# Retention and two feed-forward layers on one core: each layer's first step by eight block products, and second-stage blocks fetched four steps ahead

## The chip, the cores and the metric
The kernel runs on one core of a Trainium2 chip. The metric is the device time of the whole program in microseconds (us), median of several runs. TensorE (PE) multiplies into PSUM, VectorE (DVE), ScalarE (ACT) and GpSimd (POOL) work on SBUF, and SyncE (SP) issues nearly all DMAs, in the order in which the program names them.

## The reference
`x` is the output of a retention layer (2 batches, 8 heads, 768 positions, head size 64), laid out as 1536 tokens by 512 features. Two feed-forward layers follow, with 2048 inner features:

```
state = gamma * state + k_t (outer) v_t ;  y_t = scale * q_t . state
x  = silu(x @ w_in1) @ w_out1             # 512 -> 2048 -> 512
out = leaky_relu_0.01(x @ w_in2) @ w_out2
```
All in fp32; the weights reach the kernel as 64-bit words.

## The kernel before, in words
**Retention** runs as 12 chunks of 128 positions (`j`): `queries` and `keys` scale on POOL, `scores` and `values` multiply on PE, `masked` masks on DVE, `store_x` writes the chunk into `x`. `load_att` fetches four chunks ahead.

**Numbers.** A matrix product is made of three products of high and low parts (`TERMS`): `halves(h, l, s)` makes the high part on ACT and the low part on DVE. A weight block is **converted** from its words in pieces: `words` (ACT, two instructions), `clamp` (DVE, two), `signed` (DVE, which also calls for the next load), `low` (DVE). It then lies in one of three tiles `r` (the list `rt`), and is written to a scratch in DRAM (`keep_w`, read back by `fetch_w`) or split at once. `sums` makes four sums of a block on POOL into the tile `sf`; `split_a` and `split_s` split the block and its sums.

**First stage of a layer** (x times w_in, 8 steps, `Step`): the 1536 tokens lie in four sets of 384. Set 0 and set 2 (`xa[0]`, `xa[1]`) are the upper, set 1 and set 3 (`xb[0]`, `xb[1]`) the lower halves of two pairs; index `p` (a lane) is the pair. A step does a two by two block product by seven block products instead of eight (Winograd's scheme), six matmuls of 128x384 for each product and lane. Four of the seven need the transformed inputs `T4` (`tt`), which `rest_t` (POOL) and `split_t` (ACT, DVE) make, two need the split sums. Each product adds to another in PSUM, so copies (`copy`, ACT) and adds (`add`, DVE) stand between them. `begin` runs step 0 product by product and lane by lane, and the first product of step 1 inside it; `rest` runs the steps after it, in which the next step's first product stands ahead. `up_tasks` puts conversions and splits between the products. `keep` writes a step's results (1.5 MB) to DRAM.

**Second stage** (times w_out): three groups of 512 tokens by 8 blocks of results, 24 steps `n`, each of 24 matmuls of 128x512 (`down`). `fetch_g` brings a block back into one of the three tiles `ct`, `split_g` splits it two steps ahead of its use. `todo` spreads the conversions of later weights over these steps. `finish_x` (layer 0) turns a group's PSUM into the next layer's x, `finish_out` (layer 1) stores it.

Order on each engine is that of the program text; engines wait for each other by semaphores alone. Every DMA named above but the first constants is on SP's queue.

Of the kernel before, what the change touches and what calls it, by code (L numbers as in the profile page):

```python
# [28 lines left out]
N = 384  # L29
# [12 lines left out]
def retention_moe_kernel(ctx: ExitStack, tc: tile.TileContext, att, w1, w2, cst, out):  # L42
# [28 lines left out]
    rt = [sb.tile([128, 2, 512], I32, name=f"r{i}") for i in range(3)]  # L71
    u = sb.tile([128, 2, 512], I32, name="u")
    sf = sb.tile([128, 4, 256], F32, name="sf")
# [212 lines left out]


# [52 lines left out]
    A22, A11, A12 = range(3)  # L340
# [24 lines left out]
    class Step:  # L365
# [46 lines left out]
        def done(self):  # L412
            free.extend(W.pop(self.w))
# [5 lines left out]
    def fetch_g(layer, s, i):  # L419
        n = len(fetched)  # L420
        fetched.append(n)
        t = sf.rearrange("p (a b) n -> p a (b n)", a=2) if n % (SETS * Q) == 0 else ct[(n % (SETS * Q) - 1) % 3]
# [34 lines left out]
    with tc.manual_schedule():  # L457
        nc.scalar.dma_start(out=cs, in_=cst[:, 0:ncs])
        g2 = rt[2][0:1].bitcast(F32)
# [50 lines left out]
        def pieces(w, end=keep_w):  # L510
# [6 lines left out]
            8: lambda: (low(wa), sums(wa, (0,)), split_t(0, 0)), 9: lambda: (sums(wa, (1,)), split_a(wa)),  # L517
            10: lambda: (sums(wa, (2, 3)), rest_t(0), words(wb)), 11: lambda: (split_s(wa), rest_t(1)),
        }
        for j in range(NJ):  # L520
# [25 lines left out]
        def up_tasks(layer, k):  # L546
            t = [[] for _ in range(8)]
            at = lambda n, *f: t[n].extend(f)
            if layer == 0 and k < 2:
                wd = first_w[3]  # L550
                if k == 0:
                    at(0, lambda: split_t(1, 0))
                    at(1, lambda: split_t(0, 1))
                    at(2, lambda: clamp(wb))
                    at(3, lambda: signed(wb), lambda: split_t(1, 1))
                    at(4, lambda: (low(wb), sums(wb)))
                    at(5, lambda: split_a(wb), lambda: words(wc))
                    at(6, lambda: clamp(wc))
                    at(7, lambda: split_s(wb))
                else:  # L560
                    at(0, lambda: signed(wc))
                    at(1, lambda: (low(wc), sums(wc)), lambda: words(wd))
                    at(2, lambda: split_a(wc))
                    at(3, lambda: split_s(wc), lambda: clamp(wd))
                    at(5, lambda: signed(wd))
                    at(6, lambda: (low(wd), sums(wd)))
# [24 lines left out]
            if k == 0:  # L591
                at(0, lambda: split_t(1, 0))
# [199 lines left out]
```

## Time and profile before

| | us |
|---|---|
| median of 3 runs (628.49 to 631.32) | 629.25 |
| the profiled execution | 629.81 |
| its span, first to last instruction | 628.0 |
| PE busy / mean granted clock | 572.3 / 0.959 |
| DVE busy, ACT busy, POOL busy | 341.3, 286.0, 107.6 |

The profiled execution lies 0.56 us above the median, and its span is 1.81 us shorter than its time. Busy time of PE counts pipelined matmuls and can hide slow ones; the stages have to be read one by one.

### The profile page before, as it was taken

Reading aid. Unit: us, or ns where it says so; the run is one execution under the profiler, and the core shown is the slowest. Engines: PE = TensorE matmul, PEld = TensorE weight load, DVE = VectorE, ACT = ScalarE, POOL = GpSimd, SP = SyncE. Lnnn points to the kernel's source line nnn. Section 1 sums busy time; section 2 is a strip of 40 time slices with the busy share of each in tenths; the row PEclk is TensorE's granted clock in tenths of the full one; section 3 lists DMA queues with packets and bytes.
Section 4 is the critical chain, followed back from the end, with each engine's and each line's share of the span. In section 5 each row is a group of like instructions: output and inputs, shape, how many; then the busy total and the mean of one; then the engine's idle time right before and its main releaser. Section 6 shows DMA issues by size and latency. Waiting matters only on the chain.

```text
span 628.0 us, 7949 instructions
## 1 busy us (share of the span) xinstructions
PE 572.3 (91%) x3222; PEld 503.5 (80%) x3222; DVE 341.3 (54%) x359; ACT 286.0 (46%) x337; POOL 107.6 (17%) x102
## 2 busy tenths in 40 slices
PE   9968699999998699899989788999999699999996
PEld 7757589998997487687767688999998488888884
DVE  4974846887864375545755756556655361320400
ACT  2222447777763544424634365665565341422301
POOL 2746314333300000000204522212200000000000
PEclk9997879999999799899999798999999899999999
DMA  8980106787757755676557206677735770631501
GB/s 328 380 303 3 67 3 232 255 280 264 273 194 255 256 168 176 225 223 211 170 188 240 109 0 238 238 253 251 254 139 201 280 262 26 235 100 48 187 1 67
DMA packets 35129, 119.09 MB, mean 190 GB/s; under 512 B 3218, under 2 KB 3346, under 8 KB 33044
## 3 DMA queue, kind: packets, MB, share of 16 engines
q1 hardware_dynamic: 34800, 118.24, 54.3%
q8 instruction: 25, 0.41, 0.2%
q10 hardware_dynamic: 292, 0.34, 0.2%
q14 instruction: 12, 0.10, 0.1%
HBM read 80.82 MB, written 37.75 MB: 189 GB/s over the span
## 4 chain that ended last, share of the span: by engine, by line
PE 52%; DMA 16%; DVE 14%; ACT 8%; issue 6%; POOL 3%; SPq 1%; ACTq 0%; DVEq 0%; POOLq 0%
PE p L436 25%; PE p L359 23%; DMA c<-g 9%; DMA scr<-r 3%; ACT w L172 3%; DVE w L173 2%; DVE r L142 2%; DVE r L149 2%; DVE big L392 2%; POOL sf L169 1%; DMA att_b<-att_dram 1%; DVE r L131 1%; DMA sf<-g 1%; DVE tt L173 1%; ACT u L127 1%
## 5 line engine op out<-in xcount | busy, mean ns | idle before, releaser
L359 PE MATMUL p<-tt,w 128*128 128x384 f32 x768 | 149.9, 346 | 13.4 <-ACT c L388 8.3
L359 PEld LDWEIGHTS p<-tt,w 128*128 128x128 f32 x768 | 139.3, 194 | 17.5 <-ACT c L388 11.2
L173 DVE TENSOR_TENSOR w<-c,w 128x1024 fp32r<-128x1024 f32 x46 | 56.8, 1236 | 137.0 <-ACT w L172 136.9
L436 PE MATMUL p<-w,wt 128*128 128x512 f32 x432 | 105.7, 404 | 10.8 <-ACT wt L172 5.0
L436 PEld LDWEIGHTS p<-w,wt 128*128 128x128 f32 x432 | 83.2, 194 | 33.2 <-DVE w L173 5.8
L436 PE MATMUL p<-wt,w 128*128 128x512 f32 x432 | 101.8, 397 | 7.6 <-ACT wt L172 6.0
L436 PEld LDWEIGHTS p<-wt,w 128*128 128x128 f32 x432 | 82.4, 191 | 26.6 <-ACT wt L172 6.4
L172 ACT ACTIVATE w<-c 128x1024 fp32r<-128x1024 f32 x46 | 48.7, 1061 | 107.4 <-DMA c<-g 70.0
L359 PE MATMUL p<-xa,w 128*128 128x384 f32 x384 | 74.4, 342 | 5.7 <-ACT c L388 5.3
L359 PEld LDWEIGHTS p<-xa,w 128*128 128x128 f32 x384 | 68.7, 192 | 6.9 <-ACT c L388 5.9
L436 PE MATMUL p<-w,w 128*128 128x512 f32 x288 | 69.2, 398 | 3.4 <-ACT w L172 1.8
L388 ACT ACTIVATE c<-p 128x768 f32<-128x768 f32 (+1 forms) x54 | 39.8, 741 | 65.8 <-PE p L359 63.2
L436 PEld LDWEIGHTS p<-w,w 128*128 128x128 f32 x288 | 54.9, 192 | 16.7 <-DVE w L173 2.8
L392 DVE TENSOR_TENSOR big<-p,c 128x768 f32<-128x768 f32 (+1 forms) x54 | 46.7, 864 | 39.4 <-PE p L359 23.3
L169 POOL TENSOR_TENSOR sf<-r 128x256 f32<-128x256 f32 x32 | 36.6, 1164 | 172.9 <-DVE r L149 64.9
L127 ACT ACTIVATE u<-ws 128x1024 int32<-128x1024 uint32 x32 | 36.5, 1140 | 16.2 <-DVE r L149 16.2
L149 DVE CUSTOM_DVE_ANT_0 r<-r,u 128x2048 uint16<-128x2048 uint16 x32 | 41.2, 1287 | 1.1
L125 ACT ACTIVATE r<-ws 128x1024 f32<-128x1024 f32 x32 | 36.5, 1139 | 9.3 <-DMA scr<-r 9.2
L142 DVE SCALAR_TENSOR_TENSOR r<-ws,r 128x1024 int32<-128x1024 int32 x32 | 39.6, 1237 | 0.4
L173 DVE TENSOR_TENSOR w<-sf,w 128x1024 fp32r<-128x1024 f32 x18 | 22.4, 1246 | 29.4 <-ACT w L172 29.4
L359 PE MATMUL p<-xb,w 128*128 128x384 f32 x192 | 37.3, 342 | 0.0
L359 PEld LDWEIGHTS p<-xb,w 128*128 128x128 f32 x192 | 34.6, 192 | 0.0
(74 smaller groups left out, 457.1 us busy)
## 6 DMA issues: line engine op xcount, KB each, us to landing
ws<-w_dram SPq DMA_DIRECT2D x64, 512.0 KB, 5.4
g<-big SPq DMA_DIRECT2D x16, 1536.0 KB, 5.8
c<-g SPq DMA_DIRECT2D x46, 512.0 KB, 6.8
att_a<-att_dram SPq DMA_DIRECT2D x18, 512.0 KB, 7.0
scr<-r SPq DMA_DIRECT2D x18, 512.0 KB, 6.4
r<-scr SPq DMA_DIRECT2D x18, 512.0 KB, 7.3
att_b<-att_dram SPq DMA_DIRECT2D x6, 512.0 KB, 8.4
out_dram<-big SPq DMA_DIRECT2D x11, 256.0 KB, 2.1
```

Of the source, the lines that this page charges most:

```text
L125: nc.scalar.activation(out=r.bitcast(F32), in_=t[:, :, :, 1].bitcast(F32), func=AF.Abs)
L127: nc.scalar.activation(out=u, in_=t[:, :, :, 0].bitcast(U32), func=AF.Copy, scale=2.0 ** -29)
L131: nc.vector.tensor_scalar(out=r.bitcast(F32), in0=r.bitcast(F32), scalar1=MIN_NORMAL, scalar2=MAX_NORMAL, op0=ALU.max, op1=ALU.min,)
L142: nc.vector.scalar_tensor_tensor(out=r, in0=t[:, :, :, 1], scalar=-0x40000000, in1=r, op0=ALU.bitwise_and, op1=ALU.bitwise_or)
L149: nc.vector.tensor_tensor(out=r, in0=r, in1=u, op=ALU.add)
L169: nc.gpsimd.tensor_tensor(out=o, in0=a, in1=b, op=op)
L172: nc.scalar.activation(out=h, in_=s, func=AF.Copy)
L173: nc.vector.tensor_tensor(out=l, in0=s, in1=h.bitcast(F32), op=ALU.subtract)
L359: nc.tensor.matmul(out=o, lhsT=a[:, ta, k * 128:k * 128 + 128], rhs=rhs(p, tb, k), start=(begin and m == 0), stop=(end and m == 5), skip_g ...
L388: nc.scalar.activation(out=ct[n][:, c, 0:N], in_=self.X[:, c, 0:N], func=AF.Copy)
L392: nc.vector.tensor_tensor(out=self.block(f, half, lanes), in0=t[:, c, 0:N], in1=ct[n][:, c, 0:N], op=ALU.add)
L436: nc.tensor.matmul(out=y, lhsT=l, rhs=r, start=(i == 0 and f == 0 and n == 0), stop=(i == Q - 1 and f == 1 and n == 2),)
```

## The change
Three edits. (1) Step 0 of each layer is computed by eight plain block products: four blocks for lane 0 first, then four for lane 1, twelve matmuls each, and the next step's first product at the end. It needs neither `T4` nor sums, but the split of set 1 and set 3 as they are (`b12`); these are made where x is stored (`put_second`), in tiles lent for it. The sums of the first weight block go. (2) In the second stage blocks are asked for four steps ahead (before the step's split, no longer behind it), the first four of them and two weight blocks before the last first-stage `keep`. (3) Conversions in the second stage take two steps each, on fixed steps. Beside these: the last group of layer 1 has a PSUM tile for each of its four outputs.

```diff
     def split_a(w):
...
-        halves(t[:, 0, 0:3], t[:, 1, 0:3], blocks(w)[:, 1:4])
+        b = 0 if w[2] == 0 else 1
+        halves(t[:, 0, b:4], t[:, 1, b:4], blocks(w)[:, b:4])
+        if w[2] == 0:
+            rt.append(rs.pop(w))
...
         h, l = (xb[p][:, n, :, a:b] for n in range(2))
+        halves(*(t[:, :, a:b] for t in b12[p]), ys[0])
         nc.vector.tensor_tensor(out=t[:, 0], in0=ys[0], in1=f[:, 0], op=ALU.subtract)
...
-            8: lambda: (low(wa), sums(wa, (0,)), split_t(0, 0)), 9: lambda: (sums(wa, (1,)), split_a(wa)),
-            10: lambda: (sums(wa, (2, 3)), rest_t(0), words(wb)), 11: lambda: (split_s(wa), rest_t(1)),
+            8: lambda: low(wa), 9: lambda: split_a(wa),
+            10: lambda: (rest_t(0), words(wb)), 11: lambda: (rest_t(1), clamp(wb), signed(wb)),
...
+                    at(0, lambda: split_t(0, 0), lambda: low(wb))
+                    at(1, lambda: sums(wb), lambda: split_t(1, 0))
+                    at(2, lambda: split_a(wb))
+                    at(3, lambda: split_t(0, 1), lambda: words(wc))
+                    at(4, lambda: split_s(wb))
+                    at(5, lambda: split_t(1, 1))
+                    at(6, lambda: clamp(wc), lambda: signed(wc))
+                    at(7, lambda: low(wc), lambda: sums(wc))
...
+        def begin(s, n, tasks, tags, second_half, put_back):
...
+            blocks_ = [(0, 0), (1, 0), (0, 1), (1, 1)]
+            for p in range(2):
+                for at, m in enumerate(second_half if p else range(4)):
+                    f, half = blocks_[m]
+                    for t in tasks[4 * p + at]:
+                        t()
...
+                    for kk in range(4):
+                        r = (A11, A21)[f] + kk // 2
+                        for ta, tb in TERMS:
+                            if half == 0:
+                                x = xa[p][:, tb, kk]
+                            elif kk < 2:
+                                x = b12[p][tb][:, kk]
+                            else:
+                                x = xb[p][:, tb, kk - 2]
...
+                    if p == 1:
+                        s.act(f, half, places[m])
+                put_back[p]()
+            n.go(1)
+            n.copy(0)
...
             steps[Q - 1].act(0, 1)
+            fetch_g(layer, 0, 3)
             steps[Q - 1].keep()
-            fetch_g(layer, 0, 2)
...
-            tags = [((2, 0), (1, 3), (2, 0)), ((3, 1), (0, 2), (3, 1))][layer]
+            tags = [((2, 0), (1, 3), (2, 0)), ((3, 1), (0, 2), (3, 1, 0, 2))][layer]
...
+                if n + 4 < SETS * Q:
+                    fetch_g(layer, *divmod(n + 4, Q))
                 if n + 2 < SETS * Q:
                     split_g(layer, *divmod(n + 2, Q))
-                if n + 3 < SETS * Q:
-                    fetch_g(layer, *divmod(n + 3, Q))
```

GpSimd at the end of retention, before (`L213` is `queries`, `L218` `keys`, `L225` `decay`, `L169` `sums`, `L307` and `L308` `rest_t`):

```order
L225 TENSOR_TENSOR gst<-gst,cs 128x256
L169 TENSOR_TENSOR sf<-r_74 128x256
L213 TENSOR_TENSOR att_a<-att_a,gst 128x512
L218 TENSOR_TENSOR att_a<-att_a,cs 128x512
L225 TENSOR_TENSOR gst<-gst,cs 128x256
L169 TENSOR_TENSOR sf<-r_74 128x256
L213 TENSOR_TENSOR att_b<-att_b,gst 128x512
L169 TENSOR_TENSOR sf<-sf,r_74 128x256
L169 TENSOR_TENSOR sf<-r_74,sf 128x256
L307 TENSOR_TENSOR big<-big 128x768
```
GpSimd at the same place in the changed kernel (`L222` `queries`, `L227` `keys`, `L234` `decay`, `L324` and `L325` `rest_t`, `L175` `sums`):

```order
L234 TENSOR_TENSOR gst<-gst,cs 128x256
L222 TENSOR_TENSOR att_a<-att_a,gst 128x512
L227 TENSOR_TENSOR att_a<-att_a,cs 128x512
L234 TENSOR_TENSOR gst<-gst,cs 128x256
L222 TENSOR_TENSOR att_b<-att_b,gst 128x512
L324 TENSOR_TENSOR big<-big 128x768
L325 TENSOR_TENSOR big<-big 128x768
L324 TENSOR_TENSOR big<-big 128x768
L325 TENSOR_TENSOR big<-big 128x768
L175 TENSOR_TENSOR sf<-r_75 128x256 x2
```
The four sums of the first weight block no longer stand between the last chunks' queries.

PE where layer 0's first step begins, before (`tt` are the transformed inputs, `p_654` and the like PSUM tiles, each row one product of one lane):

```order
L359 MATMUL p_654<-xa_64,w_86 128x384 x6
L359 MATMUL p_662<-xa_64,w_86 128x384 x6
L359 MATMUL p_654<-xa_65,w_86 128x384 x6
L359 MATMUL p_654<-tt_85,w_87 128x384 x6
L359 MATMUL p_662<-xa_65,w_86 128x384 x6
L359 MATMUL p_695<-tt_85,w_87 128x384 x6
L359 MATMUL p_654<-tt_85,w_87 128x384 x6
L359 MATMUL p_695<-tt_649,w_87 128x384 x6
```
PE at the same place in the changed kernel (`w_86` and `w_87` now hold the split of sets 1 and 3, `w_88` the weights):

```order
L648 MATMUL p_661<-xa_64,w_88 128x384 x12
L648 MATMUL p_662<-xa_64,w_88 128x384 x12
L648 MATMUL p_663<-w_86,w_88 128x384 x6
L648 MATMUL p_663<-xb_66,w_88 128x384 x6
L648 MATMUL p_664<-w_86,w_88 128x384 x6
L648 MATMUL p_664<-xb_66,w_88 128x384 x6
L648 MATMUL p_662<-xa_65,w_88 128x384 x12
L648 MATMUL p_661<-xa_65,w_88 128x384 x12
```
No row reads `tt` any more, and each block has a PSUM tile of its own with no add between them.

SP where layer 0 goes over to its second stage, before (`L408` is `keep`, `L424` `fetch_g`, `L159` `fetch_w`, `L119` a load of words):

```order
L408 DMA g_6_1559<-big 128x3072
L424 DMA sf<-g_0_831 128x2x512
L119 DMA ws_73<-w_dram 128x1024 x2
L424 DMA c_69<-g_1_949 128x2x512
L159 DMA r_74<-scr_1_2_1026 128x1024
L408 DMA g_7_1632<-big 128x3072
L424 DMA c_70<-g_2_1074 128x2x512
L424 DMA c_71<-g_3_1199 128x2x512
L159 DMA r_75<-scr_1_3_1151 128x1024
```
SP at the same place in the changed kernel (`L425` `keep`, `L441` `fetch_g`, `L165` `fetch_w`, `L125` words):

```order
L425 DMA g_6_1565<-big 128x3072
L441 DMA sf<-g_0_841 128x2x512
L441 DMA c_69<-g_1_955 128x2x512
L125 DMA ws_73<-w_dram 128x1024 x2
L165 DMA r_74<-scr_1_2_1032 128x1024
L441 DMA c_71<-g_2_1080 128x2x512
L165 DMA r_75<-scr_1_3_1157 128x1024
L441 DMA c_70<-g_3_1205 128x2x512
L425 DMA g_7_1641<-big 128x3072
L441 DMA c_69<-g_4_1330 128x2x512
```
Blocks 2 and 3 and the second weight block moved from behind the last `keep` to before it.

## Rows read from the trace of the kernel before
**Rows 1.** Stretches: length, busy (count) by engine, granted clock, DMA share, GB/s.
```profile
61.38:105.86 44.48, 37.06 (x182) 34.83 (x181) 29.47 (x31) 25.96 (x34) 10.68 (x11) 0.88 0.24 87
105.86:195.65 89.79, 86.67 (x493) 85.71 (x492) 68.50 (x71) 62.86 (x73) 24.60 (x20) 1.00 0.75 257
195.65:349.92 154.27, 140.79 (x576) 111.34 (x577) 86.85 (x86) 64.66 (x67) 10.18 (x6) 0.96 0.63 208
349.92:394.89 44.97, 36.71 (x182) 34.81 (x180) 26.15 (x28) 24.27 (x33) 14.80 (x14) 0.89 0.31 104
482.08:628.00 145.92, 134.59 (x577) 109.21 (x576) 38.01 (x32) 40.02 (x45) 0.00 (x0) 0.98 0.37 130
```
**Rows 2.** PE in order of time: start, length, count, [idle before, releaser].
```profile
457.81 4.35 PE L359 MATMUL p<-tt,w 128*128 128x384 f32 x24
472.49 4.35 PE L359 MATMUL p<-tt,w 128*128 128x384 f32 x24
477.80 2.35 PE L359 MATMUL p<-tt,w 128*128 128x384 f32 x12 [0.96 <-ACT c L388]
546.02 32.80 PE L436 MATMUL p<-wt,w 128*128 128x512 f32 x144
578.66 11.04 PE L436 MATMUL p<-w,w 128*128 128x512 f32 x48
```
**Rows 3.** End of retention in order of time, all engines.
```profile
32.81 0.98 SPq L209 DMA_DIRECT2D att_a<-att_dram  x2
...
45.01 2.17 POOL L169 TENSOR_TENSOR sf<-r 128x256 f32<-128x256 f32 x1 [7.87 <-DVE r L149]
47.14 1.26 POOL L213 TENSOR_TENSOR att_a<-att_a,gst 128x512 f32<-128x512 f32 x1
...
48.45 2.08 PE L235 MATMUL p<-att_a 64*128 64x128 f32 x16 [6.84 <-POOL att_a L213]
...
54.95 1.16 PE L235 MATMUL p<-att_b 64*128 64x128 f32 x16
```
**Rows 4.** Layer 0's first step in order of time.
```profile
64.33 2.82 POOL L308 TENSOR_TENSOR big<-big 128x768 f32<-128x768 f32 x1
...
65.38 3.39 DVE L173 TENSOR_TENSOR tt<-big,tt 128x1536 fp32r<-128x1536 f32 x1
...
69.15 1.74 DVE L173 TENSOR_TENSOR tt<-big,tt 128x1536 fp32r<-128x1536 f32 x1
...
76.02 4.21 PE L359 MATMUL p<-tt,w 128*128 128x384 f32 x12 [3.31 <-DVE big L392]
```
**Rows 5.** Layer 0's second stage begins, in order of time.
```profile
203.16 0.33 SPq L408 DMA_DIRECT2D g<-big  x1
...
210.81 1.06 ACT L172 ACTIVATE w<-c 128x1024 fp32r<-128x1024 f32 x1 [7.68 <-DMA c<-g]
...
212.87 1.22 PE L436 MATMUL p<-w,wt 128*128 128x512 f32 x2 [5.01 <-ACT wt L172]
```
**Rows 6.** From the page: costliest groups (busy, mean ns | idle), and DMA issues (KB, us to landing).
```profile
L173 DVE TENSOR_TENSOR w<-c,w 128x1024 fp32r<-128x1024 f32 x46 | 56.8, 1236 | 137.0 <-ACT w L172 136.9
...
L172 ACT ACTIVATE w<-c 128x1024 fp32r<-128x1024 f32 x46 | 48.7, 1061 | 107.4 <-DMA c<-g 70.0
...
c<-g SPq DMA_DIRECT2D x46, 512.0 KB, 6.8
```
**Rows 7.** Layer 1's first steps in order of time.
```profile
352.92 0.81 ACT L172 ACTIVATE xb<-p 128x768 fp32r<-128x768 f32 x1 [1.54 <-DVE big L302]
...
353.77 0.96 DVE L173 TENSOR_TENSOR xb<-p,xb 128x768 fp32r<-128x768 f32 x1 [0.88 <-ACT xb L172]
...
389.13 3.83 PE L359 MATMUL p<-tt,w 128*128 128x384 f32 x12 [2.56 <-ACT c L388]
```
**Rows 8.** Layer 1's second stage, PE in order of time.
```profile
499.47 1.22 PE L436 MATMUL p<-wt,w 128*128 128x512 f32 x2 [5.99 <-ACT wt L172]
...
618.94 3.01 PE L436 MATMUL p<-wt,w 128*128 128x512 f32 x12 [0.69 <-ACT big L454]
```

More of the change, by code (lines that the diff above doesn't have):

```diff
@@ L285, in state, with place @@
             nc.vector.tensor_tensor(out=s0, in0=s1, in1=uu, op=ALU.add)
+    b12 = [None, None]
+    def place(p):
+        t = free.pop(0)
+        b12[p] = [t[:, n, :, 0:N] for n in range(2)]
+        return t
     def put_first(s, a, b, ys):
@@ L412, in done @@
         def done(self):
-            free.extend(W.pop(self.w))
+            free.extend(t for t in W.pop(self.w) if t is not None)
     gf, gh = {}, {}
@@ L665, in rest @@
             s.done()
+        put_back = [lambda p=p: free.append(places[p]) for p in range(2)]
         for layer in range(2):
@@ L672, in retention_moe_kernel @@
                 if k == 0:
-                    begin(s, n, tasks)
+                    begin(s, n, tasks, ((0, 1, 2, 3), (1, 3, 0, 2))[layer],
+                          ((1, 0, 2, 3), (2, 0, 1, 3))[layer], put_back)
                     s.done()
@@ L704, in retention_moe_kernel, with again @@
                 if i == 0:
[L705 to L706 removed]
+                    if len(tags[s]) == 2:
+                        ya, yb = (pair(t) for t in tags[s])
+                        ys = [ya[:, 0], ya[:, 1], yb[:, 0], yb[:, 1]]
+                    else:
+                        ys = [pair(t)[:, 0] for t in tags[s]]
+                if n == 7 and layer == 0:
+                    spare = next(k for k in range(3) if any(t is rs_all[k] for t in rt))
+                    rt[:] = [t for t in rt if t is not rs_all[spare]]
+                    b12[0] = [sb.tile([128, 2, N], FR, tag=t, name="b12") for t in ("sf", f"r{spare}")]
+                    def again(k=spare):
+                        nonlocal sf
+                        sf = sf_tile()
+                        rs_all[k] = rt_tile(k)
+                        rt.append(rs_all[k])
+                    put_back[0] = again
+                if n + 4 < SETS * Q:
+                    fetch_g(layer, *divmod(n + 4, Q))
                 if n + 2 < SETS * Q:
                     split_g(layer, *divmod(n + 2, Q))
[L709 to L710 removed]
                 if (layer, 1, n + 2) in scr:
                     third((layer, 1, n + 2))
[L713 to L716 removed]
+                if (layer, 1, n + 4) in scr:
+                    fetch_w((layer, 1, n + 4))
                 if layer == 0 and n == 21:
                     T4[0] = tt_tile(0)
[L719 to L724 removed]
+                for t in todo[n]:
+                    t()
+                end_ = i == Q - 1
+                if end_ and layer == 1 and s == SETS - 1:
                     for m in range(4):
@@ L729, in retention_moe_kernel @@
                     break
-                for f in range(2):
-                    for m in range(4):
-                        down(layer, s, i, f, m, ys[m])
+                if i == 0 and s:
+                    for h in range(2):
+                        for f in range(2):
+                            for m in range(2 * h, 2 * h + 2):
+                                down(layer, s, i, f, m, ys[m])
+                else:
+                    for f in range(2):
+                        for m in range(4):
+                            down(layer, s, i, f, m, ys[m])
                 free.append(gh.pop((layer, s, i)))
@@ L735, in retention_moe_kernel @@
                     free.append(W.pop((layer, 1, i)))
-                if end and layer == 0:
+                if end_ and layer == 0:
+                    if s == 2:
+                        last_place = place(1)
+                        put_back[1] = lambda: free.append(last_place)
                     finish_x(s, ya, yb)
```

130 lines of the change are left out of this document (55 added, 75 removed).

## The prediction
> **What bounds the kernel now.** I read the stretches first [rows 1], since PE's 91% busy share hides which stage loses what. For the losses I need PE's pace when nothing holds it, from its rows in order of time [rows 2]: from 457.81 to 472.49 lie 84 matmuls of 384 columns, so 14.68 / 84 = 0.1748 us each; from 546.02 to 578.66 lie 144 of 512 columns, 0.2267 us each. Against that pace the stretches give:
>
> - layer 0, steps 0 and 1 (61.38 to 105.86): 96 + 84 = 180 matmuls, 31.5 us at pace, 44.48 taken, 13.0 lost;
> - layer 0, steps 2 to 7: 492 matmuls, 86.0 at pace, 89.79 taken, 3.8 lost;
> - layer 0, second stage: 576 matmuls, 130.6 at pace, 154.27 taken, 23.7 lost;
> - layer 1, steps 0 and 1: 31.5 at pace, 44.97 taken, 13.5 lost;
> - layer 1, second stage: 130.6 at pace, 145.92 taken, 15.3 lost, some of it the last store behind the last matmul.
>
> PE is thus the bound wherever it is fed, and the time to be won lies in five places where it is not. What starves it I read from the rows around each gap. At the end of retention PE waits 6.84 us for POOL, and POOL has itself waited 7.87 us with a sum that needs the weight block's last piece on DVE; the chunk's queries stand behind that sum [rows 3]. In layer 0's first step PE waits for adds and copies between chained products, 3.31 us at 76.02, because DVE is busy with `tt` splits ahead of the add [rows 4]. In the second stages SP holds the fetches: the last `keep` of layer 0 is issued at 203.16, the fetch behind it lands at 210.81 after ACT has idled 7.68 us, and PE stands 5.01 us [rows 5]; in layer 1 the same wait is 5.99 us [rows 8].
>
> **The change part by part.**
>
> *End of retention.* Four sums leave POOL's order. The queries of chunk 10 then wait only for their data: issued at 32.81 to 33.79 [rows 3], and a block of the same 512 KB takes 6.8 us to land [rows 6], so 40.6; plus 1.26 for the scaling gives 41.9, where PE was free at 48.45 - 6.84 = 41.6. So the wait falls from 6.84 to about 0.3. At 48.45 a group of 16 takes 2.08 us and at 54.95 the same group 1.16 [rows 3]: PE ran at its lower clock (1.2 instead of 2.4 GHz) after the wait. I count three groups at 0.9 us, an estimate from that one pair, so 2.7. Against this: `b12` adds six ACT and six DVE pieces of a quarter block in `put_second`, and the last mask on DVE stands behind a split of a whole weight block, 1.24 us [rows 6], in place of three quarters of one; and the last chunk's data, asked for behind chunk 10's, now sets the pace. I take 1.5 us for these together. The first block product starts 6.5 + 2.7 - 1.5 = **7.7 us** earlier, at 53.7; the bounds are 5 (no clock gain) and 9.3.
>
> *Layer 0, steps 0 and 1.* The step has 96 + 12 matmuls instead of 84 + 12, so the two steps are 192 at pace, 33.6 us. No product of step 0 waits for an add. One wait is new: step 1's first product is the last of `begin`, and `copy` must read it before the next product adds onto it. The same neighbourhood stands once in the trace, at 477.80, and cost 0.96 us [rows 2]; I take 1.0. DVE and ACT must finish splits of `tt`, of the second block and its sums, and convert the third, within these 34.6 us. In the old stretch DVE was busy 29.47 and ACT 25.96 of 44.48 us [rows 1]; of DVE's work six half-size adds of step 0 go, so some 27 us must fit in 34.6. It fits with a microsecond to spare where it matters: `copy` of step 1's third product stands on ACT behind the split of the third block's sums. Gain 44.48 - 34.6 = **9.9 us**, with 4 as the lower bound (rival A).
>
> *Layer 0, second stage.* Fetches 2 and 3 are issued before the last `keep` (203.16 [rows 5]), each as soon as the last step's adds have read its tile. After that each fetch waits only until its tile has been split, one step earlier than before. The loop of a tile is 6.8 to land, 1.06 to split high and 1.24 low [rows 6], 9.1 us, and it has three steps of 24 x 0.2267 = 5.44 us, 16.3. So fetches should not be late. A DMA share of 0.63 [rows 1] in this stretch leaves room for the shorter time: the same bytes in 132 us make 0.73. The conversions' `keep_w` still stands between fetches on SP and waits for DVE, but with two steps of slack rather than one. I leave 2.0 us lost, an allowance for the entry and for conversions that meet the first splits, of 23.7: **21.7 us**; bounds 12 and 23.
>
> *Layer 1, steps 0 and 1.* Lane 0's first two blocks have free PSUM tiles. The third takes the tile that `finish_x` reads last. In the old kernel that read ended with the low part of `xb` at 353.77 + 0.96 = 354.73 [rows 7]. The new `b12` split of the same 128x768 comes ahead of it, 0.81 on ACT and 0.96 on DVE one after the other [rows 7], plus up to 0.6 until ACT reaches it: 356.5 to 357.1. At pace the third block is due 24 matmuls after 349.92, at 354.1. So PE **stands 2.9 us in a place where it did not**. After a wait of 2.56 us the trace has 12 matmuls in 3.83 us instead of 2.35 [rows 7, 2], the lower clock again, so 1.5 more. On the other side, the wait at 389.13 itself (2.56 and 1.5), which came from a conversion tile still being written out, goes: its conversion now starts in step 0. Total 33.6 + 1.0 + 2.9 + 1.5 = 39.0 against 44.97: **6.0 us**; bounds 3 and 10.4 (neither wait nor clock).
>
> *Layer 1, second stage.* The 5.99 us wait goes; behind it eight steps (499.47 to 546.02 [rows 8, 2]) took 46.55 us where 43.5 are due, so 3.0 for the lower clock. At the end PE waits 0.69 us [rows 8] twice for ACT to empty half of a shared PSUM tile; four tiles end that, 1.4. I leave 0.5: **9.9 us**; bounds 5 and 10.4.
>
> *At nothing:* steps 2 to 7 of both layers are the same rows at the same pace; their 3.8 us stay. The conversions' new places cost nothing while DVE has its idle time in the second stage (86.85 busy of 154.27 [rows 1]); if that cover went, the next late thing would be the split of the block two steps ahead.
>
> Sum: 7.7 + 9.9 + 21.7 + 6.0 + 9.9 = 55.2. The profiled execution took 629.81, so **574.6**; it lies 0.56 above the median of the runs, within their spread, and I state 574.5.
>
> **The rivals.**
>
> *A, VectorE becomes the bound of layer 0's first step.* While POOL's `rest_t` ran, a `tt` split took 3.39 us, and 1.74 alone [rows 4], so 1.65 more for 2.82 of POOL. POOL has about 10 us in these two steps [rows 1], nearly all beside DVE's splits now that the steps are shorter. If DVE is held for POOL's whole time instead of the 3 us that I let it lose, the third block's sums come some 6 us later, the spare is used up, and PE stands 4.5 us plus 1.5 for the clock: 580.5. For it: the 3.39. Against it: of the 2.82 only 1.65 came on top.
> The Trainium skill, "SBUF — State Buffer", section "SBUF: two separate sides", says that VectorE with two SBUF inputs and GpSimd hold their shared port for a whole instruction and the other is blocked outright; by it this rival would be the case, at 580.5. The 3.39 us row agrees in kind and not in full (1.65 of 2.82).
>
> *B, the fetches stay late.* SP still takes everything in order, and weight loads and write-outs wait on DVE between the fetches. With two results of 1.5 MB and some eight blocks of 512 KB on the queue at the entry, landing could take 10 us instead of 6.8; the steps behind the first weight blocks have about 1 us of slack. If half of the loss stays in both second stages, 15.8 comes back: 590.
>
> *C, the chunk's data is the bound at the end of retention, not POOL* (the change does not do what it seems to there). SP's load at 32.81 speaks for it; were it to land 5 us later than I count, the clock falls as before: 580.
>
> *D, slower than before.* The loop of a fetched tile, 9.1 us, decides: if landing took over 15.2 us instead of 6.8, the loop would exceed its three steps by 1.2 us, and 46 fetches would give back 55 us: 630 and up. The longest that ACT idled for a fetch in these rows is 7.68 us [rows 5].
>
> *E, better:* no wait and no lower clock at layer 1's start: 570.
>
> **How the numbers follow.** Forecast 0.66, with a range of its own of 570 to 581 from the bounds above; A 0.11, B 0.11, C 0.05, D 0.02, E 0.05. The range 567 to 588 leaves out D, the greater part of B and the outer ends. Every case but D is faster by far more than 0.5%, which is about what a measurement of this kernel can tell: faster 0.97, within 0.5% 0.01, slower 0.02.
>
> **What would show it.** PE's first block product should start near 53.7, without a wait for queries over 1 us; between it and step 2 some 34.6 us, one wait of about 1 us for `copy`. The second stages should take about 132.6 us and 136, with no wait of PE over 1.5 us. At layer 1's third block PE should wait about 2.9 us for DVE. Wrong would be: a PE wait over 3 us for `copy` or an add in step 1 (A), waits for `split_g` with ACT idle on a fetch (B), POOL waiting over 3 us on chunk 10 or 11 (C).

## The result, and the profile after

The changed kernel takes 579.5 us (median; 578.59 to 581.96) against 629.8 us, a ratio of 0.921 with an interval of 0.917 to 0.925. The prediction said 574.5 us in a range of 567 to 588. The profiled execution took 580.35 us with a span of 578.6; the one before had a span of 628.0.

The stretches of the changed kernel, in the columns of [rows 1]; its first block product starts at 58.67, step 2 at 98.50, the second stage of layer 0 at 186.59, layer 1 at 318.36, its step 2 at 355.94, its second stage at 443.14:

```profile
0.00:58.67 58.67, 49.37 (x727) 41.08 (x727) 42.98 (x65) 17.10 (x31) 30.94 (x32) 0.94 0.74 271
58.67:77.83 19.16, 17.03 (x98) 16.70 (x96) 15.54 (x13) 9.64 (x11) 10.66 (x6) 1.00 0.16 55
77.83:98.50 20.67, 19.77 (x96) 19.25 (x97) 14.10 (x14) 14.07 (x17) 5.52 (x7) 0.83 0.52 173
98.50:186.59 88.09, 86.43 (x493) 85.69 (x492) 68.39 (x71) 62.14 (x72) 22.21 (x18) 1.00 0.73 255
186.59:318.36 131.77, 131.00 (x577) 108.25 (x577) 85.51 (x87) 64.43 (x68) 3.65 (x2) 1.00 0.72 241
318.36:355.94 37.58, 34.02 (x193) 33.40 (x192) 24.54 (x21) 22.48 (x27) 16.36 (x14) 1.00 0.36 126
443.14:578.60 135.46, 131.35 (x577) 107.81 (x576) 38.99 (x33) 40.04 (x45) 0.00 (x0) 0.99 0.40 138
```

Set against [rows 1], stage by stage in us (a gain is time that the stage no longer takes):

| stage | before | after | gain | predicted gain |
|---|---|---|---|---|
| up to the first block product | 61.38 | 58.67 | 2.7 | 7.7 |
| layer 0, steps 0 and 1 | 44.48 | 39.83 | 4.7 | 9.9 |
| layer 0, steps 2 to 7 | 89.79 | 88.09 | 1.7 | 0 |
| layer 0, second stage | 154.27 | 131.77 | 22.5 | 21.7 |
| layer 1, steps 0 and 1 | 44.97 | 37.58 | 7.4 | 6.0 |
| layer 1, second stage | 145.92 | 135.46 | 10.5 | 9.9 |

The second stages gave what was predicted, and two thirds of the whole. The two places ahead of 98.50 gave 7.4 instead of 17.6. What PE waits for is now (line waited for, us in total, times, longest; after, the longest four):

```profile
PE p L264 <- DVE c L251: 7.0, 4, 2.8
PE p L376 <- ACT c L405: 3.7, 4, 1.0
PE p L648 <- DVE xb L179: 2.7, 1, 2.7
PE p L376 <- ACT big L418: 2.1, 1, 2.1
```

No wait for POOL's queries is left (6.84 in [rows 3]) and none over 1 us in the second stages (5.01 and 5.99 in [rows 5, 8]). The 0.9 us waits for `copy` (L405) and the 2.7 us at layer 1's third block (L648) are the two that the prediction announced. The first line, `values` waiting for a mask on DVE, it had only inside an allowance of 1.5 us, and the fourth, step 1's first product waiting for an activation, not at all. In the kernel before the masks cost this:

```profile
PE p L255 <- DVE c L242: 1.8, 2, 1.2
```

In PE's rows of the end of retention (after; start, duration, what it waited for) the 16 matmuls of L264 take 1.09 us at 33.02 and 1.98 at 55.16; the granted clock is 0.55 of full speed from 55.16 to 58.67, nearly all of it at the lower level, and 0.60 from 34.05 to 38.31, behind the wait at 33.02:

```profile
33.02 1.09 PE L264 MATMUL p<-c,att_a 128*64 128x128 f32 x16 [2.24 <-DVE c L251]
55.16 1.98 PE L264 MATMUL p<-c,att_b 128*64 128x128 f32 x16 [2.76 <-DVE c L251]
```

DVE's rows beside POOL's (after) show why the masks (L251) are late:

```profile
27.99 1.53 DVE L179 TENSOR_TENSOR w<-sf,w 128x256 fp32r<-128x256 f32 x1 [0.48 <-ACT w L178]
29.45 1.26 DVE L318 TENSOR_TENSOR big<-sf,big 128x256 f32<-128x256 f32 x1
31.75 1.22 DVE L251 TENSOR_TENSOR c<-p,c 128x1024 f32<-128x1024 f32 x1
33.22 0.41 DVE L318 TENSOR_TENSOR big<-p,big 128x256 f32<-128x256 f32 x1
46.89 2.20 DVE L155 CUSTOM_DVE_ANT_0 r<-r,u 128x2048 uint16<-128x2048 uint16 x1
52.74 1.23 DVE L179 TENSOR_TENSOR w<-r,w 128x1024 fp32r<-128x1024 f32 x1 [0.20 <-ACT w L178]
53.88 1.22 DVE L251 TENSOR_TENSOR c<-p,c 128x1024 f32<-128x1024 f32 x1
```
```profile
27.96 1.28 POOL L222 TENSOR_TENSOR att_b<-att_b,gst 128x512 f32<-128x512 f32 x1 [1.49 <-DMA att_b<-att_dram]
32.48 1.28 POOL L222 TENSOR_TENSOR att_a<-att_a,gst 128x512 f32<-128x512 f32 x1
```

The new low part of `b12` (27.99) falls beside a POOL operation and takes 1.53 us; the same shape takes 0.41 where one operand is in PSUM (33.22, also beside POOL). The next subtraction takes 1.26 for the same reason, and the mask is issued at 31.75. At the end the mask stands behind the store of a chunk with its `b12` piece and the split of the whole weight block (52.74). One more delay lies a step ahead of it: `low` of the first block (46.89) takes 2.20 us beside POOL's `rest_t` (46.20 to 50.77), where the same instruction takes 1.23 at 83.58 with POOL idle, and from there to the last mask DVE idles no more than 0.65 us.

In layer 0's first step the chain runs through POOL (POOL's, ACT's and PE's rows of after, in that order):

```profile
69.37 3.60 POOL L175 TENSOR_TENSOR sf<-r 128x256 f32<-128x256 f32 x2 [4.69 <-DVE r L155]
72.94 2.25 POOL L175 TENSOR_TENSOR sf<-sf,r 128x256 f32<-128x256 f32 x1
75.26 0.73 POOL L175 TENSOR_TENSOR sf<-r,sf 128x256 f32<-128x256 f32 x1
76.03 1.06 ACT L178 ACTIVATE w<-sf 128x1024 fp32r<-128x1024 f32 x1 [2.40 <-POOL sf L175]
76.99 0.79 ACT L418 ACTIVATE big<-p 128x768 f32<-128x768 f32 x1
77.83 3.44 PE L376 MATMUL p<-xa,w 128*128 128x384 f32 x12 [2.14 <-ACT big L418]
82.18 3.91 PE L376 MATMUL p<-tt,w 128*128 128x384 f32 x12 [0.90 <-ACT c L405]
```

The second block's sums take 6.6 us on POOL (69.37 to 75.99) where four sums with no split beside them take 3.0 (96.56 to 99.52), ACT holds their split until they are done, and the activation that empties PE's next PSUM tile stands behind that split. PE waits 2.14 us, and its next two products take 3.44 and 3.91 us where 2.25 is the pace: the granted clock is 0.58 from 77.83 to 86.00.

### The profile page after: what moved, and what is told of

Its sections match the earlier page's. It is cut to its first block, busy times and chain, and to the rows that moved or that the text cites. A ratio compares the mean times of both kernels' runs of the same rounds, so it can differ in the third digit from the quotient of the medians.

```text
span 578.6 us, 7971 instructions
## 1 busy us (share of the span) xinstructions
PE 555.2 (96%) x3246; PEld 498.1 (86%) x3246; DVE 342.6 (59%) x354; ACT 282.7 (49%) x330; POOL 104.4 (18%) x94
## 4 chain that ended last, share of the span: by engine, by line
PE 83%; DVE 6%; DMA 5%; ACT 3%; POOL 1%; issue 1%; SPq 0%; DVEq 0%; ACTq 0%
PE p L453 44%; PE p L376 33%; DMA sf<-g 3%; DMA att_a<-att_dram 3%; PE p L648 2%; DVE w L179 2%; POOL sf L175 1%; PE p L273 1%; PE p L264 1%; ACT w L178 1%; PE p L244 1%; DVE c L251 1%; DVE r L155 1%; DVE big L318 1%; DVE big L319 1%
## 5 line engine op out<-in xcount | busy, mean ns | idle before, releaser
L376 PE MATMUL p<-tt,w 128*128 128x384 f32 x672 | 126.3, 340 | 3.7 <-ACT c L405 3.7
L376 PEld LDWEIGHTS p<-tt,w 128*128 128x128 f32 x672 | 119.4, 190 | 5.3 <-ACT c L405 5.2
L453 PE MATMUL p<-w,wt 128*128 128x512 f32 x432 | 98.4, 389 | 0.0
L376 PE MATMUL p<-xa,w 128*128 128x384 f32 x336 | 64.3, 341 | 2.1 <-ACT big L418 2.1
L376 PEld LDWEIGHTS p<-xa,w 128*128 128x128 f32 x336 | 59.8, 190 | 2.5 <-ACT big L418 2.5
L409 DVE TENSOR_TENSOR big<-p,c 128x768 f32<-128x768 f32 x42 | 40.1, 954 | 32.3 <-PE p L376 19.8
L405 ACT ACTIVATE c<-p 128x768 f32<-128x768 f32 x42 | 34.1, 812 | 48.7 <-PE p L376 48.6
L175 POOL TENSOR_TENSOR sf<-r 128x256 f32<-128x256 f32 x28 | 33.9, 1232 | 115.6 <-DVE r L155 61.1
L133 ACT ACTIVATE u<-ws 128x1024 int32<-128x1024 uint32 x32 | 36.4, 1137 | 22.5 <-DVE r L155 22.5
L179 DVE TENSOR_TENSOR w<-sf,w 128x1024 fp32r<-128x1024 f32 (+1 forms) x18 | 21.7, 1205 | 32.8 <-ACT w L178 32.8
L148 DVE SCALAR_TENSOR_TENSOR r<-ws,r 128x1024 int32<-128x1024 int32 x32 | 39.6, 1236 | 0.7
L324 POOL TENSOR_TENSOR big<-big 128x768 f32<-128x768 f32 x4 | 7.3, 1832 | 169.1 <-DVE big L319 169.1
L179 DVE TENSOR_TENSOR w<-r,w 128x768 fp32r<-128x768 f32 (+1 forms) x20 | 23.5, 1175 | 14.5 <-ACT w L178 14.5
```

The costliest lines, as they stand in the source:

```text
L133: nc.scalar.activation(out=u, in_=t[:, :, :, 0].bitcast(U32), func=AF.Copy, scale=2.0 ** -29)
L148: nc.vector.scalar_tensor_tensor(out=r, in0=t[:, :, :, 1], scalar=-0x40000000, in1=r, op0=ALU.bitwise_and, op1=ALU.bitwise_or)
L175: nc.gpsimd.tensor_tensor(out=o, in0=a, in1=b, op=op)
L179: nc.vector.tensor_tensor(out=l, in0=s, in1=h.bitcast(F32), op=ALU.subtract)
L376: nc.tensor.matmul(out=o, lhsT=a[:, ta, k * 128:k * 128 + 128], rhs=rhs(p, tb, k), start=(begin and m == 0), stop=(end and m == 5), skip_g ...
L405: nc.scalar.activation(out=ct[n][:, c, 0:N], in_=self.X[:, c, 0:N], func=AF.Copy)
```

## Experiments

Each ran beside the kernel before on the same chip; medians, with the ratio to it. "Stage" numbers are from PE's rows, as in the table above.

**The second stages: fetch order and conversions.** e1 puts the fetches back, e2 only the last `keep`, e3 only the conversions; e4 puts the new fetch order alone into the kernel before.

e1, the loop (the entry's fetches and weight blocks go back likewise):

```diff
-                if n + 4 < SETS * Q:
-                    fetch_g(layer, *divmod(n + 4, Q))
                 if n + 2 < SETS * Q:
                     split_g(layer, *divmod(n + 2, Q))
+                if n + 3 < SETS * Q:
+                    fetch_g(layer, *divmod(n + 3, Q))
```

e2:

```diff
-                    tasks[4] += [lambda: split_g(layer, 0, 0), lambda: fetch_g(layer, 0, 2)]
+                    tasks[4] += [lambda: split_g(layer, 0, 0)]
...
+            steps[Q - 1].keep()
+            fetch_g(layer, 0, 2)
             fetch_g(layer, 0, 3)
-            steps[Q - 1].keep()
```

e3, in place of the loop that spreads them:

```diff
+                packed = []
+                for w in second_w[0][6:] + first_w[Q:]:
+                    packed += pieces(w, end)
+                for n in range(21):
+                    todo[n] += packed[n * len(packed) // 21:(n + 1) * len(packed) // 21]
```

e4 takes the new fetch order of the change, loop, entry and the order in which the tiles `ct` are used, into the kernel before.

> The changed kernel with the order of the fetches in both second stages as it was: three steps ahead and behind the split, the last keep ahead of the third fetch, one weight block ahead. Conversions stay spread over two steps. Theory (the fetch order alone is the term of 21.7 + 9.9 us of the prediction): the two second stages take some 153 and 145 us again, waits of PE of 5 to 6 us at each entry, total 579.5 + 31.6 = 611 us. Rival (the loss came mostly from conversions packed into one step, whose write-outs stand on SP between the fetches; they are still spread here): total under 597 us, with most of the gain kept in layer 0's stage.

> The changed kernel with only the entry undone: the third and fourth fetch stand on SP behind the last keep of the first stage; inside the stage everything is four steps ahead. Theory (the entry is a loss of its own, since keep must wait for the last adds and activations): PE stands 3 to 6 us once in each second stage and runs some us at the lower clock behind it; total 579.5 + 2 x 5.5 = 590.5 us. Rival (fetching four ahead makes up for the late start, one step of slack being 5.4 us): within 3 us of the changed kernel, under 583 us.

> The changed kernel with the conversions of layer 0's second stage packed again as before (four pieces in a row, 40 pieces over 21 steps) and nothing else undone. Theory (prediction: conversions cost nothing, DVE has idle time): total within 2 us of the changed kernel, 578 to 582 us. Rival (spreading them is what lets DVE and SP through): PE waits for split tiles in layer 0's second stage, total 585 to 592 us.

> The kernel before with only the fetch order of the change in both second stages (four steps ahead, ahead of the split, two weight blocks ahead, ring order, last keep behind the fourth fetch). First steps and conversions as before. Theory: it brings the 21.7 + 9.9 us of the prediction by itself, 629 - 31.6 = 597.5 us. Rival (needs the spread conversions too): 603 to 612 us.

| kernel | median us | ratio | layer 0, second stage | layer 1, second stage |
|---|---|---|---|---|
| before | 628.4 | | 154.3 | 145.9 |
| changed | 579.5 | 0.921 | 131.8 | 135.5 |
| e1, fetches back | 621.6 | 0.990 (0.985 to 0.995) | 163.7 | 144.5 |
| e2, keep first | 595.7 | 0.948 (0.943 to 0.954) | 138.0 | 143.2 |
| e3, conversions back | 580.6 | 0.924 (0.919 to 0.929) | 131.7 | 135.4 |
| e4, before + fetches | 596.0 | 0.949 (0.944 to 0.954) | 133.3 | 136.8 |

The line of the changed kernel is from the result above, with its own runs of the kernel before. e4 settles the term: the order alone brings 32.4 us, with the old first steps and the old conversions, where 31.6 were forecast. It leaves layer 1's last group with the old PSUM tiles, still waits 1.4 us there, and takes 136.8 us in that stage instead of 135.5: the 1.4 us came as costed. e3 shows that the spread conversions are worth nothing beside the new order. e2 shows that the entry is a loss of its own, 16.2 us in the median, 14 of it in the two stages (6.2 and 7.7); its PE rows at the two entries:

```profile
201.97 1.22 PE L453 MATMUL p<-w,wt 128*128 128x512 f32 x2 [2.84 <-ACT wt L178]
467.22 1.22 PE L453 MATMUL p<-wt,w 128*128 128x512 f32 x2 [5.88 <-ACT wt L178]
```

e1 was 10 us slower than its theory had it, and all of that in layer 0: with the spread conversions the old order is worse than before (163.7 against 154.3). In layer 1, which converts nothing, e1 takes 1.3 us more than e2, so that the order inside the stage counts beside the conversions and hardly without them. Rows of e1 (DVE's, SP's, ACT's, PE's) show how a fetch comes late there:

```profile
237.27 1.23 DVE L148 SCALAR_TENSOR_TENSOR r<-ws,r 128x1024 int32<-128x1024 int32 x1
238.56 0.81 SPq L125 DMA_DIRECT2D ws<-w_dram  x2
239.46 0.53 SPq L441 DMA_DIRECT2D c<-g  x1
247.85 1.06 ACT L178 ACTIVATE w<-c 128x1024 fp32r<-128x1024 f32 x1 [5.87 <-DMA c<-g]
248.96 0.50 PE L453 MATMUL p<-w,w 128*128 128x512 f32 x1 [2.05 <-ACT w L178]
```

The fetch (L441) stands on SP behind a weight load (L125), which waits for `signed` (L148) on DVE, which stands behind the split of a tile fetched before (234.68). It lands 8.3 us later; ACT has idled 5.87 us for it, and PE waits. The two longest waits of PE inside the stage, 2.57 us at 258.27 and 3.36 at 313.13, are less direct: ACT's split stands there behind the pieces of `finish_x`, which wait for DVE behind a late split and a conversion. The loads still stand between the fetches in the new order (SP waits 79.1 us for `signed` in the changed kernel's stage), but each fetch is asked for a step earlier. ACT's idle time for fetched tiles in layer 0's second stage is 49.0 us before, 60.5 in e1, 26.9 in e4 and 19.4 in the changed kernel. Why e1 is worse than before is not shown by a run of its own.

**The end of retention.** e5 moves two `b12` pieces behind the last mask and the last mask ahead of a store and a split.

```diff
+        if j in (3, 4) and not W_DONE:
+            later.append(lambda: halves(*(t[:, :, a:b] for t in b12[p]), ys[0]))
...
+            if j + 2 == NJ - 1:
+                queries(j + 2)
+                scores(j + 2)
+                masked(j + 2)
+                state(j)
+                store_x(j)
```

> The changed kernel, end of retention alone: the b12 pieces of chunks 3 and 4 wait until after the last mask, and the last mask stands on DVE ahead of chunk 9's store and of the split of the first weight block. Theory (the 5.0 us that are missing from the term of 7.7 went to waits of values for masks, 1.33, 2.24, 0.65 and 2.76 us at 26.97, 33.02, 50.28 and 55.16, which stand on DVE behind the b12 pieces and the split, and to the lower clock behind two of them): the first block product moves from 58.67 to 53 or 54, no wait for a mask over 1.3 us, total 574 to 576 us. Rival (the waits only move to the next thing that is late, the chunks' data or POOL's scaling): the first block product stays at 57 or later, total over 578 us.

It took 579.7 us (ratio 0.922, 0.917 to 0.927). The first half of the theory held: the waits for masks fell from 7.0 to 0.6 us, and the first block product starts at 53.63. One wait of `values` of 2.08 us is left, at 50.84, without a named releaser; it ends as DVE's last read of chunk 9's PSUM tile does (50.31 + 0.42). The total did not move: the second block's sums start at 67.24, only 2.1 us earlier than in the changed kernel, and the first step hangs on them (PE's rows of e5):

```profile
53.63 5.27 PE L661 MATMUL p<-xa,w 128*128 128x384 f32 x24
75.62 3.91 PE L381 MATMUL p<-xa,w 128*128 128x384 f32 x12 [4.14 <-ACT big L423]
```

The wait for the activation grew from 2.14 to 4.14 us; step 2 starts at 95.62 instead of 98.50, and in e11, the changed kernel again, it starts at 96.50.

**Layer 0's first two steps.** e6 takes one activation ahead of the sums' split, the second block's `low` ahead of the first `tt` split, and puts the third block's conversion into step 1. e8 puts step 1's first product ahead of the last block product. e9 leaves the sums out.

e6:

```diff
-                    at(0, lambda: split_t(0, 0), lambda: low(wb))
+                    at(0, lambda: low(wb), lambda: split_t(0, 0))
...
-                    at(4, lambda: split_s(wb))
-                    at(5, lambda: split_t(1, 1))
-                    at(6, lambda: clamp(wc), lambda: signed(wc))
-                    at(7, lambda: low(wc), lambda: sums(wc))
+                    at(5, lambda: split_s(wb))
...
+                    at(0, lambda: words(wc), lambda: split_t(1, 1), lambda: clamp(wc), lambda: signed(wc))
```

e8, in `begin`:

```diff
+                    if 4 * p + at == 7:
+                        n.go(1)
+                        n.copy(0)
...
-            n.go(1)
-            n.copy(0)
```

e9:

```diff
-                    at(1, lambda: sums(wb), lambda: split_t(1, 0))
+                    at(1, lambda: split_t(1, 0))
```

> The changed kernel, layer 0's first two steps alone: low(wb) stands ahead of the first tt split, the sums' split behind one activation, the last tt split and the third block's conversion go into step 1. Theory (step 1's first product waits 2.14 us only because the activation stands on ACT behind a split that waits for POOL's sums, and the lower clock behind that wait costs some 2.8): no wait for that activation, steps 0 and 1 take 35 to 37 us instead of 39.8, total 575 to 577 us. Rival A of the prediction in another form (VectorE and POOL together are the bound, the order on ACT does not matter): the wait turns up at the next product, for the sums' split or a tt split, steps 0 and 1 stay at 39 us or more.

> The changed kernel with step 1's first product and its copy ahead of step 0's last block product, in both layers. Theory (the wait of 0.9 us at step 1's second product is for the copy alone, as the prediction put it, and a block product of 2.1 us covers it): in layer 1 the 0.90 us wait is gone and the two steps take 36.7 us; in layer 0 the wait for the activation stays, 2 us earlier in the program and some 4 us long. Total 578 us. Rival (ACT's order holds the copy in any case): the 0.9 us stay in layer 1, total 579.5 us or more.

> The changed kernel without the four sums of the second weight block on POOL (step 1's products of sums then read what stands in that tile, so this kernel leaves that part of the computation out). Theory (POOL's sums and DVE's splits of two operands in SBUF hold each other up: 6.6 us of sums beside the splits against 3.6 alone, and the splits 1.50 and 2.29 against 0.95 and 1.74): the splits take 0.95 and 1.75 us, step 1's first product does not wait for the activation, steps 0 and 1 take 35.5 to 37 us instead of 39.8, total 575 to 577 us. Rival (ACT alone is late, with its splits of 1.47 us ahead of the activations): the wait of some 2 us stays and so does the time, 579 us.

e6 took 582.8 us (0.927, 0.922 to 0.931), e8 579.6 (0.922), e9 578.1 (0.918, 0.912 to 0.924) beside 580.65 for the changed kernel on the same chip. In e6 the product at 73.80 waits for nothing, so the order on ACT did make that wait, and no clock is lost behind it; but the time comes back in waits further on (PE's rows of e6):

```profile
73.80 2.25 PE L376 MATMUL p<-xa,w 128*128 128x384 f32 x12
77.75 2.37 PE L376 MATMUL p<-tt,w 128*128 128x384 f32 x12 [1.70 <-ACT c L405]
87.68 0.62 PE L376 MATMUL p<-xa,w 128*128 128x384 f32 x2 [1.27 <-ACT w L178]
89.19 3.36 PE L376 MATMUL p<-xa,w 128*128 128x384 f32 x10 [0.90 <-DVE w L179]
```

The two steps take 41.3 us, the rival's case. In e8 layer 1 came out as the theory said (no `copy` wait, 36.4 us); in layer 0 the wait for the activation is 4.23 us and the two steps take 40.2. In e9 DVE's splits take what they take alone, and the wait shrinks to 0.91 (DVE's and PE's rows):

```profile
70.53 0.95 DVE L179 TENSOR_TENSOR w<-r,w 128x768 fp32r<-128x768 f32 x1
71.40 1.75 DVE L179 TENSOR_TENSOR tt<-big,tt 128x1536 fp32r<-128x1536 f32 x1
75.00 2.36 PE L376 MATMUL p<-xa,w 128*128 128x384 f32 x12 [0.91 <-ACT big L418]
79.18 2.35 PE L376 MATMUL p<-tt,w 128*128 128x384 f32 x12 [1.82 <-ACT c L405]
```

The same two splits take 1.50 and 2.29 us in the changed kernel (70.87 and 72.30). But even without the sums the steps take 38.0 us, 1.8 less and not the 3 to 4 of the theory: a wait for `copy` of 1.82 has come, behind the other activations on ACT, which works without a gap there.

**Layer 1's third block product.** e7 exchanges two PSUM tiles.

```diff
-((0, 1, 2, 3), (1, 3, 0, 2))[layer],
+((0, 1, 2, 3), (1, 3, 2, 0))[layer],
-((1, 0, 2, 3), (2, 0, 1, 3))[layer], put_back)
+((1, 0, 2, 3), (3, 0, 1, 2))[layer], put_back)
```

> The changed kernel with two PSUM tiles exchanged in layer 1's first step: its third block product takes the tile that finish_x reads first, the fourth the one that it reads last. Theory (the 2.67 us wait at the third block is for that tile alone): the wait falls under 1 us at either block, layer 1's steps 0 and 1 take 35.5 us instead of 37.6, total 577.5 us. Rival (the wait is for lane 0's operands or DVE's queue): it stays over 2 us.

577.9 us (0.918, 0.914 to 0.923). The wait is 0.50 us, at the fourth product, and the two steps take 36.2 us (37.6 in the changed kernel): the cause is the tile that `finish_x` reads last.

**Together, and the changed kernel again.** e10 has the edits of e5, e7 and e8, from e6 the activation ahead of the sums' split and the last `tt` split in step 1, and the second block's conversion earlier:

```diff
-            8: lambda: low(wa), 9: lambda: split_a(wa),
-            10: lambda: (rest_t(0), words(wb)), 11: lambda: (rest_t(1), clamp(wb), signed(wb)),
+            8: lambda: (low(wa), words(wb)), 9: lambda: split_a(wa),
+            10: lambda: ([f() for f in later], rest_t(0), clamp(wb), signed(wb)),
+            11: lambda: (low(wb), sums(wb), rest_t(1)),
...
-                    at(4, lambda: split_s(wb))
-                    at(5, lambda: split_t(1, 1))
+                    at(5, lambda: split_s(wb))
```

> The changed kernel with the late b12 pieces and the early mask, the second block's conversion one to two chunks earlier and its sums ahead of rest_t(1) on POOL, the first activation ahead of the sums' split on ACT, the two PSUM tiles exchanged in layer 1, and the next step's first product ahead of the last block product. Theory (the waits found are causes of their own, once the second block's conversion, on which the first step hangs, moves with the end of retention): first block product at 53 to 54, steps 0 and 1 of layer 0 in 34 to 36 us, of layer 1 in 34 to 35, total 567 to 570 us. Rival (DVE and POOL together are the bound from 45 us on, so that every microsecond won ahead is waited for behind): step 2 of layer 0 starts no earlier than 95, total 575 us or more.

> The changed kernel itself beside the other two, for their comparison on the same chip: 579.5 us, first block product between 56 and 58.7, depending on how often PE runs at the lower clock in the first 60 us.

e12 against e10:

```diff
-            11: lambda: (low(wb), sums(wb), rest_t(1)),
+            11: lambda: (rest_t(1), low(wb), sums(wb)),
...
-                at(4, lambda: sums(n), lambda: clamp(w))
-                at(5, lambda: signed(w), lambda: fetch_w(m))
+                at(4, lambda: sums(n), lambda: fetch_w(m), lambda: clamp(w))
+                at(5, lambda: signed(w))
```

> The kernel of e10 with rest_t(1) back ahead of the second block's sums on POOL, and in layer 1 the next block's fetch one place earlier. In e10 the first activation (72.81) waited for rest_t(1) on POOL, which reads the tile that the activation writes. Theory (that order was my mistake, the chain through POOL is the bound and gets 3.6 us shorter for the activation): rest_t(1) runs at 59 to 63, the sums end near 69.5, the activation comes at 67 to 69, PE waits less than 1 us for it, step 2's first product starts near 89 instead of 94.9; in layer 1 the wait of 1.64 us goes; total 570 us. Rival (DVE and POOL hold each other up, whichever comes first): the sums end after 72, PE waits 3 us or more in the first step, total 574 us or more.

e11 took 580.65 us, e10 576.2 (0.916, 0.912 to 0.920), e12 572.9 (0.912, 0.909 to 0.915). e10's theory failed and its rival's signs came (step 2 at 94.91, over 575 us). e12 beats both kernels, by 55 us and by some 7. Of the 5.4 us between its profiled span and the changed kernel's, 3.1 lie in layer 1's first stage (34.5 us for steps 0 and 1 instead of 37.6) and 2.4 ahead of layer 0's second stage. In layer 0 its theory failed (ACT's, POOL's and PE's rows of e12):

```profile
68.85 0.81 ACT L423 ACTIVATE big<-p 128x768 f32<-128x768 f32 x1 [1.33 <-DVE tt L179]
72.99 1.06 ACT L178 ACTIVATE w<-sf 128x1024 fp32r<-128x1024 f32 x1 [3.33 <-POOL sf L175]
64.86 4.48 POOL L175 TENSOR_TENSOR sf<-r 128x256 f32<-128x256 f32 x2
70.83 2.13 POOL L175 TENSOR_TENSOR sf<-r,sf 128x256 f32<-128x256 f32 x1
76.20 2.37 PE L381 MATMUL p<-tt,w 128*128 128x384 f32 x12 [1.38 <-ACT c L410]
89.25 3.53 PE L381 MATMUL p<-tt,w 128*128 128x384 f32 x12 [2.30 <-ACT c L410]
```

The activation is in time, at 68.85. The sums, begun 4.5 us earlier than in the changed kernel, take 8.1 us instead of 6.6 and end at 72.96, not at 69.5; two waits for `copy` follow, each with ACT's split of a block's sums, which waits for POOL (3.33 us at 72.99, 3.63 at 84.38), ahead of the copy. The same split stands ahead of the activation that PE waits for in the changed kernel, e5 and e8, and ahead of the copy in e6; in e10 the activation itself waits for `rest_t` on POOL. An order of ACT with that split behind the copies too was not run. Over the orders that were, the two steps stay near 40 us:

| kernel | first block product | step 2 | us between |
|---|---|---|---|
| changed / again (e11) | 58.67 / 56.10 | 98.50 / 96.50 | 39.8 / 40.4 |
| e5, masks early | 53.63 | 95.62 | 42.0 |
| e6, activation early | 56.01 | 97.35 | 41.3 |
| e9, without sums | 57.05 | 95.07 | 38.0 |
| e10, together | 54.67 | 94.91 | 40.2 |
| e12, rest_t first | 55.49 | 95.09 | 39.6 |

## Why the prediction was right, and where it was not

- **Second stages (21.7 and 9.9 predicted, 22.5 and 10.5 measured): right, mechanism and size.** e4 gets 32.4 us from the fetch order alone, e2 shows that SP's order at the entries is 14 us of the two stages, most of layer 1's term and a quarter of layer 0's, e3 that the conversions are at nothing beside the new order, as costed.
- **Layer 1, steps 0 and 1 (6.0 predicted, 7.4 measured): right.** The new wait was put at 2.9 us and is 2.67, at that product and for that engine, and e7 takes it away. The 1.5 us for the clock did not come in the profiled execution, which is the difference; in e11 it did, and the two steps took 39.1 us where 39.0 were forecast.
- **End of retention (7.7 predicted, 2.7 measured): the mechanism right, a size off.** POOL's 6.84 us wait went as worked out. The term that failed is the allowance of 1.5 us for the `b12` pieces and the whole-block split ahead of the last mask, together with the 2.7 us of clock that were to come back. The masks' waits rose from 1.8 to 7.0 us, and PE fell to the lower clock again behind them. With two of the pieces out of the way and the last mask ahead of the split (e5) the first block product starts at 53.63; the prediction had 53.7. That close a match is in part luck: e10 and e12 have the same edits there and start it at 54.67 and 55.49, and the changed kernel itself starts it at 56.10 in e11, so that the miss is 2.4 to 5.0 us.
- **Layer 0, steps 0 and 1 (9.9 predicted, 4.7 measured): the step "some 27 us must fit in 34.6" failed, and rival A describes what happened.** DVE was busy 29.6 us in the two steps (15.54 and 14.10) instead of 27, since DVE and POOL lengthen each other: the clamps beside `rest_t` took 1.75 and 2.22 us instead of twice 0.69, and the second block's sums, 6.6 us instead of the 3.0 that four take alone, are the late link. (The 3.6 of e9's expectation is read from rows at 84.95 that have a split of DVE's beside them.) Rival A expected the wait one block later and 4.5 us long with 1.5 for the clock; in the profile it is 2.14, with 2.8 for the clock, and 3.39 in e11. That the chain of DVE, POOL and ACT as a whole bounds these steps, and no single order of it, is what the last table speaks for, and it is not shown: with the first block product anywhere between 53.6 and 58.7, step 2 starts between 94.9 and 98.5, but at least one order of ACT, the split of the sums behind the copies, was not run. Which link is worth moving to break it stays open; e9 shows only that the sums by themselves are about 2 us of it.
- **Rival A's price.** The prediction held against it that of 2.82 us of `rest_t` only 1.65 came on top of DVE's split. The split began at 65.38, 1.05 us after `rest_t` (64.33 [rows 4]), so that 1.77 us of it were left to wait for, and 1.65 of these came. So the row spoke for A, and not against it.
- The two misses ahead of 98.50 make 10.2 us less, the other stages 4.4 more, mostly a stall in layer 0's steps 2 to 7 that the prediction let stay (1.7) and layer 1's start (1.4): 49.4 us gained between the profiled spans instead of 55.2. Errors of both signs met in the total: with the misses alone it would be some 584 us, inside the stated range of 567 to 588 but outside the forecast's own 570 to 581. That 579.5 lies within 1 us of rival A's 580.5 is luck too: A's place lost 5.2 us, the end of retention 5.0, and 4.4 came back elsewhere.

The Trainium skill, "SBUF — State Buffer", section "SBUF: two separate sides", calls the port that VectorE and GpSimd share an exclusive lock, which VectorE needs when it has two inputs in SBUF. The trace agrees on who is held up: 1.26 us with both operands in SBUF (29.45) and 0.41 with one in PSUM (33.22), both beside POOL. It agrees on the size too, as the rows of the second block's sums show (DVE's of after; POOL's stand above, at 69.37 and 72.94):

```profile
70.87 1.50 DVE L179 TENSOR_TENSOR w<-r,w 128x768 fp32r<-128x768 f32 x1
72.30 2.29 DVE L179 TENSOR_TENSOR tt<-big,tt 128x1536 fp32r<-128x1536 f32 x1
```

The two engines take turns, a whole instruction at a time. The second sum ends at 72.97, 0.6 us behind the split that ends at 72.37, and the third at 75.19, 0.6 behind the one that ends at 74.59; each of the two splits takes 0.55 us more than in e9.

## What to carry to other kernels

On a queue that takes everything in order, a fetch costs what the slowest thing ahead of it waits for: asking for it further ahead of its use, with buffers enough, was worth 32 of 50 us here, and nothing else in the change came near. When a wait is taken away, look at what the next engine in line does in those microseconds, row by row; here pieces of DVE of under half a microsecond alone, and one split ahead of a mask, gave back 2.4 to 5 of 8 us. Before a vector operation is costed from a row, see whether its operands lie in SBUF and what GpSimd does at that time.

## What was not expected of the hardware

- A DVE subtraction of 128x256 took 0.41 to 0.43 us alone or with one operand in PSUM, and 1.26 to 1.53 with both in SBUF beside a POOL operation. The one-input clamp of 128x1024, 0.69 alone (80.87), took 1.75 and 2.22 beside POOL's `rest_t` (61.21 and 63.00). POOL pays too: four sums took 3.0 us alone (96.56 to 99.52) and 6.6 and 8.1 beside DVE's splits.
- The same wait does not always cost the same clock. Behind the wait at layer 1's third block, of 2.67 us in one execution and 2.66 in the other, the next matmuls of PE ran at pace in the changed kernel (granted clock 1.00 from 326.49 to 329.60) and at the lower level in e11 (0.53 from 325.71 to 329.30):

```profile
326.49 1.21 PE L648 MATMUL p<-xb,w 128*128 128x384 f32 x6
```
```profile
325.71 1.94 PE L648 MATMUL p<-xb,w 128*128 128x384 f32 x6
```

  At the end of retention it is the same: behind the last wait for a mask, of 2.76 us, the granted clock was 0.55 in the changed kernel (55.16 to 58.67) and 1.00 in e7 (53.95 to 56.00). Over the nine profiled kernels with that part unchanged the first block product started between 56.0 and 58.7, which is as much as the smaller edits here are worth.
